# LSH-masked attention and a LayerNorm feed-forward block on one core: projection copies on GpSimd, warm-up products, memset gates on loads, and a new instruction order

## The chip, the core and the metric

The kernel runs on one core of a Trainium2 chip. The core has five instruction streams that run side by side and meet only at semaphores: TensorE (PE, matrix products into PSUM), VectorE (DVE), ScalarE (ACT), GpSimd (POOL) and SyncE (SP, which here does nothing but issue DMAs). The time is that of one execution on the device, in microseconds (us); the number compared is the median of the runs.

## The reference, cut to what matters

```python
# attention: q, k, v are (4, 8, 768, 64), proj is (64, 6)
q_bits = (einsum('bhsd,dk->bhsk', q, proj) > 0)
k_bits = (einsum('bhsd,dk->bhsk', k, proj) > 0)
mask = bucket(q_bits)[:, :, :, None] == bucket(k_bits)[:, :, None, :]
scores = where(mask, q @ k.T / 8, -1e9)
attn = softmax(scores);  attn_out = attn @ v
# block: x is attn_out as (4, 768, 512), w_ch1 (512, 2048), w_ch2 (2048, 512)
xn = (x - mean(x)) / sqrt(var(x) + 1e-6) * g_ln
out = x + maximum(xn @ w_ch1, 0) @ w_ch2
```

## The kernel before

The work is cut into 12 query units `u` (three blocks of 256 queries for each of the four batches) and, for attention, into 72 steps `s`: unit `s // 6`, head group `g` (four heads), key part `kp` (256 of the 768 keys). A batch's q and k come as f32 tiles `X` (one for each `g` and for q or k, `t` = 0 or 1), are transposed in blocks on DVE, cast to bf16 (`qb`, `kb`), and hashed: a product with the projection (`hf` or `hp`), then the sign as +0.5 or -0.5 (`G`). The score product adds the hash product to q times k, so that equal buckets come out far above all others and no mask is needed.

Every operation is one word of a long string, `ORDER`: its name, the engine, and its indices. The program plays the words one after the other, so the order of the words is the order of the instructions on each engine; no scheduler moves anything. In the profile a row names the line of the instruction, inside the function; below, the line where the function begins. The words that matter here:

- `lx` (L294) loads part of an `X` tile of batch 0, `LX` (L408) a whole one of a later batch, `lv` (L370) v, `lw1` and `lw2` (L359, L362) a quarter of a weight matrix each, from GpSimd's queue, with a cast to bf16.
- `tn` (L299) transposes one third of an `X` tile of batch 0 into a `tp` tile (three buffers); `ca` (L306) casts it into `qb` or `kb`.
- `ha` (L316) is the hash product of batch 0 with the block-diagonal projection `pfull` (written by `pf`, L281); `bh` (L320) takes the signs. For the query blocks that are needed later, `hc` (L326) uses the column-tiled projection `p32` instead, and `bc`, `sl`, `bi` spread the result. `hm` (L418) is the hash product of a later batch, also with `p32`; `mo` (L434) are the 16 small DMAs for each group that put its signs in place.
- `tu` (L411) and `CA` (L415) are transposes and casts of the later batches (`T`, two buffers).
- `p32` (L285) is four small copies of the projection, one for each 32 partitions. They stand on DVE.
- `S` (L447) is the score product of a step into two PSUM tiles, `E` (L464, on ACT) the exponential of each half, `A` (L467) the product with v. The first three steps take their PSUM tiles from three in rotation; all others share two, `scA` and `scB`, so that `S` of a step overwrites what `E` of the step before reads.
- `na`, `nb`, `nc`, `ce` (DVE) normalise and centre a unit, `rs` (POOL) makes the inverse deviation, `fl` a DMA transpose (`ft` and `fc` for unit 0).
- `F` (L526) and `R` are the first feed-forward product and its relu, `D` (L543) the second, `Z` the sum with x, `O` the store.
- `warm` (L289) is 32 products of ones before the first real one.
- `mem` and `pmem`, `sel`, `on`, `cv` and `su` fill constants, the spread matrix, the ones column, v in bf16 and the sums of v.

Of the kernel before, what the change touches and what calls it, by code (L numbers as in the profile page):

```python
# [19 lines left out]
mem.v lp.a tab.a lx.s.1.0.0.1 tn.v.1.0.0 lx.s.0.0.0.1 pf.v ca.p.1.0.0 warm.t ha.t.1.0.0 tn.v.0.0.0 ha.t.0.0.0  # L20
lx.s.0.1.1.3 lx.s.0.1.0.1 bh.v.1.0.0 lx.s.1.1.0.3 lx.s.0.0.1.3 tn.v.0.1.2 bh.v.0.0.0 sel.p on.p.0 tn.v.0.1.1
ha.t.0.1.2 bh.v.0.1.2 ha.t.0.1.1 bh.v.0.1.1 ca.a.0.0.0 ca.p.0.1.2 lv.s.0.0.4 on.p.1 lv.s.0.4.4 ca.p.0.1.1 tn.v.0.1.0
S.t.2.2 tn.v.1.1.0 ha.t.0.1.0 bh.v.0.1.0 ca.p.1.1.0 tn.v.1.1.1 E.a.2.0 ca.v.0.1.0 tn.v.0.0.1 E.a.2.1 S.t.1.2 E.a.1.0
ca.p.1.1.1 E.a.1.1 ha.t.1.1.1 lw1.p.3 S.t.0.2 E.a.0.0 tn.v.1.1.2 lx.s.1.0.1.3 E.a.0.1 ha.t.1.1.0 bh.v.1.1.1 pmem.p
S.t.4.2 E.a.4.0 p32.v hc.t.0.0.1 E.a.4.1 ca.a.0.0.1 bh.v.1.1.0 ha.t.1.1.2 bh.v.1.1.2 cv.p.0.0.2 tn.v.1.0.2 cv.p.0.0.0
A.t.2.2 S.t.3.2 bc.v.0.0.1 cv.p.0.4.0 E.a.3.0 sq.t.0.0 LX.s.1.0.1 E.a.3.1 tn.v.1.0.1 sl.t.0.0.1 sc.v.0.0 bi.a.0.0.1
A.t.0.2 LX.s.1.0.0 tu.v.1.0.1.0 ca.p.1.1.2 S.t.5.2 E.a.5.0 lw1.p.2 lg.s hc.t.1.0.2 E.a.5.1 tn.v.0.0.2 cv.p.0.4.2
sq.t.0.4 sc.a.0.4 A.t.1.2 na.v.0.0 LX.s.1.1.1 ca.v.1.0.1 S.t.8.2 A.t.5.2 nb.v.0.0 E.a.8.0 hc.t.0.0.2 tu.v.1.0.0.3
A.t.3.2 E.a.8.1 bc.v.0.0.2 sl.t.0.0.2 tu.v.1.0.1.3 bi.a.0.0.2 A.t.4.2 na.v.0.1 lw1.p.0 nb.v.0.1 S.t.6.2 hc.t.1.0.1
bc.v.1.0.1 E.a.6.0 bc.v.1.0.2 A.t.8.2 LX.s.1.1.0 lv.s.1.4.1 E.a.6.1 sl.t.1.0.1 bi.a.1.0.1 nc.v.0.1 lv.s.1.0.3  # L30
nc.v.0.0 S.t.7.2 A.t.6.2 ce.v.0.0 lw1.p.1 E.a.7.0 E.a.7.1 ft.t.0.0 fc.a.0.0 ce.v.0.1 sl.t.1.0.2 bi.v.1.0.2 ft.t.0.1
fc.v.0.1 S.t.9.2 tu.v.1.0.0.2 A.t.7.2 E.a.9.0 E.a.9.1 rs.p.0 lv.s.1.0.1 F.t.0.7 na.v.1.0 F.t.0.6 lw2.p.0 tu.v.1.0.1.2
R.a.0.7 R.a.0.6 nb.v.1.0 ca.v.0.0.2 tu.v.1.0.1.1 lw2.p.1 S.t.10.2 E.a.10.1 E.a.10.0 lv.s.1.4.3 lw2.p.2 tu.v.1.0.0.1
F.t.0.5 F.t.0.4 R.a.0.4 CA.v.1.0.1 A.t.9.2 tu.v.1.0.0.0 lw2.p.3 S.t.11.2 hm.t.1.0 tu.v.1.1.0.3 bt.v.1.0 mo.s.1.0.2.3
A.t.10.2 mo.s.1.0.0.2 E.a.11.0 nc.v.1.0 mo.s.1.0.2.2 E.a.11.1 tu.v.1.1.0.2 R.a.0.5 S.t.14.2 E.a.14.0 E.a.14.1
mo.s.1.0.2.1 A.t.11.2 mo.s.1.0.3.2 mo.s.1.0.1.1 F.t.0.2 R.a.0.2 na.v.1.1 nb.v.1.1 F.t.0.3 R.a.0.3 S.t.12.2
tu.v.1.1.0.1 A.t.14.2 nc.v.1.1 ce.v.1.0 ce.v.1.1 CA.p.1.0.0 tu.v.1.1.0.0 fl.s.1.0 CA.v.1.1.0 F.t.0.0 mo.s.1.0.0.1
E.a.12.0 fl.s.1.1 ca.v.1.0.2 F.t.0.1 E.a.12.1 A.t.12.2 tu.v.1.1.1.0 R.a.0.0 tu.v.1.1.1.1 mo.s.1.0.0.3 LX.s.2.0.0
R.a.0.1 mo.s.1.0.3.3 mo.s.1.0.3.0 tu.v.1.1.1.2 S.t.13.2 E.a.13.0 E.a.13.1 mo.s.1.0.0.0 D.t.0.0.0 D.t.0.0.1 D.t.0.0.2
tu.v.1.1.1.3 hm.t.1.1 S.t.16.2 E.a.16.0 bt.v.1.1 CA.p.1.1.1 mo.s.1.1.3.1 E.a.16.1 F.t.1.2 A.t.13.2 lv.s.1.0.2  # L40
mo.s.1.1.3.3 mo.s.1.0.1.3 D.t.0.0.3 R.a.1.2 lv.s.1.0.0 su.p.1.0 tu.v.2.0.0.2 S.t.15.2 E.a.15.1 mo.s.1.1.0.2
LX.s.2.0.1 mo.s.1.0.1.2 Z.v.0.0 F.t.1.4 R.v.1.4 D.t.0.1.0 D.t.0.1.1 mo.s.1.0.1.0 rs.p.1 mo.s.1.1.0.0 LX.s.2.1.0
mo.s.1.0.3.1 mo.s.1.1.2.0 tu.v.2.0.0.1 F.t.1.1 E.a.15.0 mo.s.1.0.2.0 R.a.1.1 cv.p.1.0.2 S.t.17.2 E.a.17.0 na.v.2.0
A.t.16.2 F.t.1.5 D.t.0.1.2 lv.s.1.4.2 tu.v.2.0.1.1 E.a.17.1 mo.s.1.1.3.2 mo.s.1.1.1.1 mo.s.1.1.2.2 S.t.18.2 R.v.1.5
D.t.0.1.3 mo.s.1.1.1.0 mo.s.1.1.1.2 E.a.18.1 A.t.17.2 F.t.1.0 E.a.18.0 A.t.15.2 cv.p.1.0.0 R.a.1.0 S.t.20.2 E.a.20.0
F.t.1.3 R.a.1.3 lv.s.1.4.0 cv.p.1.4.0 Z.v.0.1 E.a.20.1 tu.v.2.0.1.0 D.t.1.0.0 D.t.1.0.1 LX.s.2.1.1 nb.v.2.0 F.t.1.6
mo.s.1.1.1.3 na.v.2.1 S.t.19.2 nb.v.2.1 cv.p.1.4.2 nc.v.2.1 tu.v.2.0.0.3 R.v.1.6 mo.s.1.1.2.1 nc.v.2.0 A.t.20.2
mo.s.1.1.0.3 mo.s.1.1.0.1 on.p.2 E.a.19.1 F.t.1.7 tu.v.2.0.1.2 mo.s.1.1.2.3 tu.v.2.0.0.0 mo.s.1.1.3.0 A.t.18.2
tu.v.2.0.1.3 D.t.1.0.2 E.a.19.0 S.t.21.2 lv.s.2.0.0 R.a.1.7 D.t.1.0.3 ce.v.2.0 fl.s.2.0 ce.v.2.1 E.a.21.1 Z.v.1.0
fl.s.2.1 hm.t.2.0 bt.v.2.0 mo.s.2.0.0.1 mo.s.2.0.2.1 E.a.21.0 S.t.22.2 CA.a.2.0.0 sp.t.1.0 rs.p.2 mo.s.2.0.2.0  # L50
D.t.1.1.0 tu.v.2.1.1.0 LX.s.3.0.0 CA.p.2.0.1 mo.s.2.0.3.3 A.t.19.2 sc.a.1.0 na.v.3.0 F.t.2.0 lv.s.2.0.2 tu.v.2.1.0.0
D.t.1.1.1 mo.s.2.0.0.3 mo.s.2.0.1.3 E.a.22.0 E.a.22.1 R.a.2.0 tu.v.2.1.1.3 su.p.1.4 S.t.23.2 lv.s.2.4.3 sp.t.1.4
mo.s.2.0.1.1 D.t.1.1.2 sc.v.1.4 LX.s.3.0.1 E.a.23.0 F.t.2.1 E.a.23.1 R.v.2.1 D.t.1.1.3 mo.s.2.0.3.0 S.t.24.2 E.a.24.0
tu.v.2.1.0.1 F.t.2.5 O.s.0.3 A.t.23.2 O.s.0.1 A.t.22.2 R.v.2.5 tu.v.2.1.1.1 E.a.24.1 Z.v.1.1 F.t.2.3 R.a.2.3 S.t.26.2
E.a.26.0 lv.s.2.4.1 E.a.26.1 lv.s.2.0.3 O.s.1.3 nb.v.3.0 nc.v.3.0 lv.s.2.4.0 mo.s.2.0.3.2 A.t.21.2 tu.v.2.1.0.2
F.t.2.2 D.t.2.0.0 S.t.25.2 E.a.25.1 R.v.2.2 na.v.3.1 F.t.2.4 R.a.2.4 tu.v.2.1.0.3 CA.v.2.1.0 D.t.2.0.1 A.t.24.2
E.a.25.0 F.t.2.6 R.a.2.6 nb.v.3.1 nc.v.3.1 ce.v.3.1 S.t.29.2 lv.s.2.0.1 E.a.29.0 cv.p.2.0.2 O.s.1.1 LX.s.3.1.1
A.t.26.2 D.t.2.0.2 E.a.29.1 F.t.2.7 O.s.1.0 O.s.0.0 fl.s.3.1 S.t.28.2 R.a.2.7 tu.v.2.1.1.2 E.a.28.1 D.t.2.0.3
hm.t.2.1 ce.v.3.0 E.a.28.0 mo.s.2.0.2.3 mo.s.2.0.2.2 fl.s.3.0 Z.v.2.0 mo.s.2.0.3.1 S.t.31.2 E.a.31.1 tu.v.3.0.0.3
mo.s.2.0.0.0 lv.s.2.4.2 bt.v.2.1 E.a.31.0 A.t.25.2 su.p.2.0 mo.s.2.1.1.0 mo.s.2.1.2.0 na.v.4.0 cv.p.2.4.0 D.t.2.1.0  # L60
sp.t.2.0 A.t.29.2 sc.v.2.0 A.t.28.2 O.s.1.2 S.t.27.2 E.a.27.1 E.a.27.0 F.t.3.4 R.v.3.4 D.t.2.1.1 nb.v.4.0 CA.p.2.1.1
mo.s.2.0.1.0 F.t.3.7 R.v.3.7 S.t.30.2 nc.v.4.0 A.t.27.2 E.a.30.0 na.v.4.1 F.t.3.1 R.v.3.1 mo.s.2.1.3.1 mo.s.2.1.2.1
nb.v.4.1 nc.v.4.1 tu.v.3.0.1.1 ce.v.4.1 D.t.2.1.2 LX.s.3.1.0 E.a.30.1 ce.v.4.0 mo.s.2.1.2.3 S.t.32.2 E.a.32.0
A.t.31.2 mo.s.2.0.1.2 F.t.3.2 E.a.32.1 D.t.2.1.3 tu.v.3.0.0.2 S.t.35.2 R.a.3.2 F.t.3.0 E.a.35.0 R.v.3.0 rs.p.4
E.a.35.1 Z.v.2.1 A.t.32.2 O.s.0.2 A.t.30.2 F.t.3.6 mo.s.2.1.3.3 R.v.3.6 S.t.34.2 E.a.34.0 D.t.3.0.0 mo.s.2.1.0.2
mo.s.2.1.1.3 F.t.3.3 cv.p.2.0.0 na.v.5.0 A.t.35.2 E.a.34.1 R.v.3.3 S.t.33.2 mo.s.2.1.1.2 F.t.3.5 su.p.2.4 fl.s.4.1
E.a.33.0 rs.p.3 D.t.3.0.1 R.v.3.5 D.t.3.0.2 D.t.3.0.3 O.s.2.1 sp.t.2.4 mo.s.2.1.0.1 E.a.33.1 lv.s.3.4.3 lv.s.3.4.0
# [51 lines left out]
def kernel(  # L119
# [15 lines left out]
    nc = tc.nc  # L135
    P = 128
# [473 lines left out]
```

## Time and profile before

| | |
|---|---|
| median of 3 runs | 311.44 us (310.58 to 312.64) |
| profiled execution: time, span | 312.11 us, 310.4 us |
| PE busy | 297.2 us (96%) |
| ACT busy | 189.2 us (61%) |
| DVE busy | 175.5 us (57%) |
| POOL busy | 77.2 us (25%) |
| mean granted TensorE clock | 0.988 |

The span runs from the first to the last instruction of the profiled execution; what the run takes beyond it (1.7 us) lies around it. Busy shares are means over the span. A busy PE is not a PE at full rate: the ends of matmuls are modelled, and the clock granted to TensorE can be halved for a while.

### The profile page before, as it was taken

How to read it: one execution, taken by the hardware profiler on the slowest of the kernel's cores; microseconds unless marked ns; L12 is line 12 of the kernel's file. 1: busy time of each engine (PE TensorE's matmuls, PEld its weight loads, DVE VectorE, ACT ScalarE, POOL GpSimd, SP SyncE). 2: the span in 40 equal slices, each digit the busy share in tenths (PEclk: the TensorE clock that was granted, in tenths of full speed). 3: DMA queues.
4: the chain of work that ended last, by engine and by line, in shares of the span. 5: the costliest groups of instructions: out<-in, count | busy, mean ns of one | idle time of the engine just before them, and what ended most of it. 6: DMA issues, size and time to landing. Idle time of an engine off the chain costs nothing.

```text
span 310.4 us, 9968 instructions
## 1 busy us (share of the span) xinstructions
PE 297.2 (96%) x4410; PEld 206.2 (66%) x4410; DVE 175.5 (57%) x353; ACT 189.2 (61%) x211; POOL 77.2 (25%) x95
## 2 busy tenths in 40 slices
PE   7959899999999999999999999999999999999995
PEld 6636677666756767766776766676776676676663
DVE  3784964933865966836867634436474246356112
ACT  2475778766685786666866677557667577332220
POOL 3590055017270152630100005096101001001000
PEclk9998979999999999999999999999999999999999
DMA  6999979148446955130252222420310311103122
GB/s 194 373 303 229 301 124 178 40 138 254 134 65 221 264 121 162 44 88 2 55 94 73 20 55 57 84 55 5 87 36 2 85 38 34 36 2 82 55 68 68
DMA packets 30426, 33.58 MB, mean 108 GB/s; under 512 B 15536, under 2 KB 27056, under 8 KB 30384
## 3 DMA queue, kind: packets, MB, share of 16 engines
q1 hardware_dynamic: 25792, 28.50, 33.5%
q0 software_dynamic: 4224, 4.19, 8.5%
q8 instruction: 34, 0.56, 0.8%
q10 hardware_dynamic: 368, 0.26, 0.3%
q14 instruction: 8, 0.07, 0.1%
HBM read 27.53 MB, written 6.29 MB: 109 GB/s over the span
## 4 chain that ended last, share of the span: by engine, by line
PE 85%; DVE 6%; DMA 3%; POOL 2%; ACT 2%; issue 1%; SPq 0%; DVEq 0%
PE f L531 26%; PE sc L459 16%; PE acc L474 11%; PE hf L318 3%; DMA X<-in_q_dram 3%; PE hp L423 2%; ACT E L465 2%; DVE T L242 1%; DVE p L287 1%; POOL qb L251 1%; PE f_01None L547 1%; PE f_80None L547 1%; PE f_31None L547 1%; PE f_101None L547 1%; PE f_100None L547 1%; PE f_20None L547 1%
## 5 line engine op out<-in xcount | busy, mean ns | idle before, releaser
L465 ACT ACTIVATE E<-sc,bias_sb 128x1024 bf16<-128x1024 f32 x144 | 153.6, 1111 | 71.8 <-PE sc L459 71.8
L531 PE MATMUL f<-xnT,w_sb 128*128 128x256 bf16 x768 | 99.4, 273 | 0.3 <-DVE B L245 0.3
L531 PEld LDWEIGHTS <-w_sb 128*128 128x128 bf16 x768 | 71.1, 98 | 20.9 <-issue 6.1
L547 PEld LDWEIGHTS <-hb 128*128 128x128 bf16 x400 | 37.1, 98 | 31.7 <-issue 3.8
L541 DVE TENSOR_SCALAR hb<-f 128x512 bf16<-128x512 f32 x45 | 31.0, 688 | 44.8 <-PE f L531 44.4
L459 PE MATMUL sc<-qb,kb 32*128 32x256 bf16 x1152 | 53.7, 271 | 0.3 <-issue 0.3
L539 ACT ACTIVATE hb<-f 128x512 bf16<-128x512 f32 x51 | 30.3, 596 | 31.9 <-PE f L531 30.2
L474 PEld LDWEIGHTS <-E 128*128 128x128 bf16 x1152 | 42.0, 99 | 8.0 <-issue 4.8
L474 PE MATMUL acc<-vaug,E 128*128 128x65 bf16 x1152 | 46.0, 195 | 0.0
L459 PE MATMUL sc<-G 6*128 6x256 bf16 x576 | 42.9, 276 | 1.4 <-ACT E L465 1.4
L509 POOL TENSOR_SCALAR rs<-mv 128x2 f32<-128x2 f32 x12 | 7.1, 593 | 103.5 <-DVE mv L503 103.2
L242 DVE STREAM_TRANSPOSE T<-X 128x384 f32<-128x384 f32 x48 | 26.1, 561 | 12.0 <-POOL qb L251 4.2
L459 PEld LDWEIGHTS <-kb 32*128 32x128 bf16 x1152 | 30.8, 95 | 2.4 <-issue 0.5
L459 PEld LDWEIGHTS <-G 6*128 6x128 bf16 x576 | 15.6, 92 | 21.9 <-issue 19.9
L487 DVE SCALAR_TENSOR_TENSOR y<-vsB,acc 128x520 f32<-128x520 f32 x24 | 16.5, 688 | 16.8 <-PE acc L474 14.8
L376 POOL CAST vaug<-vn 128x768 bf16<-128x768 f32 x16 | 13.3, 851 | 37.3 <-DMA vn<-in_v_dram 20.6
L384 POOL TENSOR_TENSOR t<-vn 128x768 f32<-128x768 f32 x6 | 10.9, 1810 | 40.7 <-DMA G<-B 33.0
L504 DVE SCALAR_TENSOR_TENSOR xc<-x,mv,gB 128x512 bf16<-128x512 f32 x24 | 19.7, 820 | 0.9
L500 DVE BATCH_NORM_STATS2 st<-x 128x6 f32<-128x256 f32 x48 | 17.5, 414 | 0.4
L496 DVE TENSOR_TENSOR x<-y,rc 128x512 f32<-128x512 f32 x24 | 16.8, 699 | 1.1 <-DVE rc L494 0.3
L318 PE MATMUL hf<-tp,pfull 128*128 128x256 f32 x32 | 10.4, 469 | 1.6 <-DVE pfull L283 1.2
L242 DVE STREAM_TRANSPOSE tp<-X 128x256 f32<-128x256 f32 x24 | 9.0, 417 | 3.0 <-DMA X<-in_q_dram 2.8
(107 smaller groups left out, 244.1 us busy)
## 6 DMA issues: line engine op xcount, KB each, us to landing
out_dram<-x SPq DMA_DIRECT2D x44, 128.0 KB
X<-in_k_dram SPq DMA_DIRECT2D x7, 768.0 KB
X<-in_q_dram SPq DMA_DIRECT2D x6, 768.0 KB
vn<-in_v_dram SPq DMA_DIRECT2D x24, 192.0 KB
w_sb<-in_moe_w_ch_dram POOLq DMA_DIRECT2D x8, 512.0 KB, 10.6
vn<-in_v_dram SPq DMA_DIRECT2D x2, 768.0 KB
G<-B SPq DMA_DIRECT2D x96, 4.5 KB
X<-in_q_dram SPq DMA_DIRECT2D x2, 512.0 KB
```

Of the source, the lines that this page charges most:

```text
L242: nc.vector.transpose(d[:, j], s[:, j, kj0 : kj0 + n])
L318: nc.tensor.matmul(hf(g, t, kp)[:, :256], pfull[:, j], tp(g, t, kp)[:, j], start=(j == 0), stop=(j == 1))
L459: nc.tensor.matmul(sc(s, i // 2)[:, i % 2, 256 * kk : 256 * kk + 256], lh, rh, start=(rep == 0), stop=(rep == 2), skip_group_check=True,)
L465: nc.scalar.activation(E(s)[:, heads(h)], sc(s, h), AF.Exp, scale=EXP_SCALE, bias=bias_sb)
L474: nc.tensor.matmul(acc[:, qt, (D + 1) * i : (D + 1) * (i + 1)], E(s)[:, i, 256 * kk + P * qt : 256 * kk + P * qt + P], vaug(u // 3)[:, 4 * ...
L496: nc.vector.tensor_tensor(xo, a[:, :, :, 0:D], rc.to_broadcast([P, 2, 4, D]), op=AOP.mult)
L500: nc.vector.bn_stats(stats(u)[:, qt, g], xt(u)[:, qt, 256 * g : 256 * g + 256])
L504: nc.vector.scalar_tensor_tensor(xc(u)[:, t], xt(u)[:, t], mv(u)[:, t, 0:1], gB, op0=AOP.subtract, op1=AOP.mult,)
L531: nc.tensor.matmul(f1[:, n].rearrange("p (t x) -> p t x", t=2), w1_sb[:, dt, P * nt : P * nt + P], xnT(u)[:, :, dt], start=(dt == 0), stop ...
L539: nc.scalar.activation(hb(u)[:, 2 * p : 2 * p + 2], f1, AF.Relu)
L541: eng.tensor_scalar_max(hb(u)[:, 2 * p : 2 * p + 2], f1, 0.0)
L547: nc.tensor.matmul(f2, hb(u)[:, nt, P * t : P * t + P], w2_sb[:, nt, half(h)], start=(nt == 0), stop=(nt == NNT - 1),)
```

## The change

`wm` is a new word: four more products of ones into the PSUM tile of `warm`. Eight of them stand among the first hash products. `gx` is a new word: a memset of one column of an `X` tile, on POOL or DVE; it stands ahead of each of the four loads `LX` of batch 1, which overwrite the same tile and so wait for the memset. `p32` stands on POOL. The whole order is new; its beginning is shown, once as it was (first lines) and once as it is, and no other function is touched. The line numbers of the new file are 1 higher in the order's wake, 5 higher behind `wm` and 8 higher behind `gx`.

```diff
 ORDER = """
-mem.v lp.a tab.a lx.s.1.0.0.1 tn.v.1.0.0 lx.s.0.0.0.1 pf.v ca.p.1.0.0 warm.t ha.t.1.0.0 tn.v.0.0.0 ha.t.0.0.0
-lx.s.0.1.1.3 lx.s.0.1.0.1 bh.v.1.0.0 lx.s.1.1.0.3 lx.s.0.0.1.3 tn.v.0.1.2 bh.v.0.0.0 sel.p on.p.0 tn.v.0.1.1
-ha.t.0.1.2 bh.v.0.1.2 ha.t.0.1.1 bh.v.0.1.1 ca.a.0.0.0 ca.p.0.1.2 lv.s.0.0.4 on.p.1 lv.s.0.4.4 ca.p.0.1.1 tn.v.0.1.0
-S.t.2.2 tn.v.1.1.0 ha.t.0.1.0 bh.v.0.1.0 ca.p.1.1.0 tn.v.1.1.1 E.a.2.0 ca.v.0.1.0 tn.v.0.0.1 E.a.2.1 S.t.1.2 E.a.1.0
-ca.p.1.1.1 E.a.1.1 ha.t.1.1.1 lw1.p.3 S.t.0.2 E.a.0.0 tn.v.1.1.2 lx.s.1.0.1.3 E.a.0.1 ha.t.1.1.0 bh.v.1.1.1 pmem.p
-S.t.4.2 E.a.4.0 p32.v hc.t.0.0.1 E.a.4.1 ca.a.0.0.1 bh.v.1.1.0 ha.t.1.1.2 bh.v.1.1.2 cv.p.0.0.2 tn.v.1.0.2 cv.p.0.0.0
+mem.v lp.a tab.a lx.s.0.0.0.1 lx.s.0.1.1.3 lx.s.0.1.0.1 lx.s.1.0.0.1 lx.s.1.1.0.3 lv.s.0.0.4 warm.t wm.t.0 wm.t.1
+tn.v.0.0.0 lx.s.0.0.1.3 ca.a.0.0.0 wm.t.2 pf.v tn.v.0.1.2 ca.p.0.1.2 wm.t.3 wm.t.4 lg.s ha.t.0.0.0 bh.v.0.0.0 wm.t.5
+wm.t.6 on.p.0 ha.t.0.1.2 tn.v.0.1.1 ha.t.0.1.1 lx.s.1.0.1.3 ca.p.0.1.1 bh.v.0.1.2 tn.v.0.1.0 S.t.2.2 lv.s.0.4.4
+E.a.2.0 wm.t.7 E.a.2.1 bh.v.0.1.1 p32.p ha.t.0.1.0 bh.v.0.1.0 S.t.1.2 E.a.1.0 gx.p.1.0.1 tn.v.1.1.1 ha.t.1.1.1
+lw1.p.3 E.a.1.1 ca.v.0.1.0 bh.v.1.1.1 tn.v.1.0.0 S.t.0.2 ca.p.1.1.1 ca.p.1.0.0 ha.t.1.0.0 LX.s.1.0.1 E.a.0.0
+tn.v.1.1.0 ha.t.1.1.0 bh.v.1.0.0 S.t.4.2 E.a.0.1 cv.p.0.0.0 cv.p.0.0.2 E.a.4.0 tn.v.0.0.1 hc.t.0.0.1 lw1.p.2
+tn.v.1.1.2 bh.v.1.1.0 E.a.4.1 ca.a.0.0.1 bc.v.0.0.1 A.t.0.2 ca.v.1.1.0 ha.t.1.1.2 sel.p lv.s.1.4.1 gx.v.1.0.0
+bh.v.1.1.2 S.t.3.2 sq.t.0.0 lv.s.1.4.2 E.a.3.0 tn.v.0.0.2 E.a.3.1 LX.s.1.0.0 sl.t.0.0.1 A.t.1.2 bi.a.0.0.1 tn.v.1.0.2
+ca.p.1.1.2 S.t.5.2 hc.t.1.0.2 A.t.2.2 ca.v.1.0.2 lw1.p.0 cv.p.0.4.2 cv.p.0.4.0 tn.v.1.0.1 lw1.p.1 lv.s.1.0.2
+ca.p.1.0.1 sc.v.0.0 na.v.0.0 E.a.5.0 ca.p.0.0.2 lv.s.1.0.0 sq.t.0.4 E.a.5.1 S.t.8.2 sc.a.0.4 hc.t.0.0.2 E.a.8.0
+tu.v.1.0.1.2 A.t.4.2 E.a.8.1 A.t.3.2 nb.v.0.0 bc.v.0.0.2 A.t.5.2 bc.v.1.0.2 gx.p.1.1.1 lv.s.1.0.3 sl.t.0.0.2
...
+LX.s.1.1.1 E.a.6.1 S.t.7.2 sl.t.1.0.2 nc.v.0.1 lw2.p.0 lw2.p.2 bi.v.1.0.1 A.t.6.2 E.a.7.0 ce.v.0.0 bi.v.1.0.2
+ft.t.0.0 ce.v.0.1 ft.t.0.1 fc.v.0.0 E.a.7.1 fc.v.0.1 S.t.9.2 E.a.9.0 tu.v.1.0.0.3 A.t.7.2 gx.v.1.1.0 F.t.0.6
...
+    def wm(eng, n):
+        for _ in range(4):
+            nc.tensor.matmul(made["warm"][:, 0, :P], ones, ones, start=True, stop=True)
+
...
+    def gx(eng, b, g, t):
+        eng.memset(Xt(b, g, t)[:, 0:1], 0.0)
```

In numbers of words, over the whole program: `S`, `E`, `A`, `F`, `R`, `D`, `O`, `mo`, `tu` and the loads are as many as before, and each as often on its engine; of the twelve `CA`, seven stand on DVE (four before), four on POOL (five) and one on ACT (three).

## The prediction

> **What bounds the kernel now.** I read the page first: the busy shares, and the span in slices. PE and the granted clock are:
>
> ```profile
> span 310.4 us, 9968 instructions
> PE 297.2 (96%) x4410; PEld 206.2 (66%) x4410; DVE 175.5 (57%) x353; ACT 189.2 (61%) x211; POOL 77.2 (25%) x95
> ...
> PE   7959899999999999999999999999999999999995
> ...
> PEclk9998979999999999999999999999999999999999
> ```
>
> PE is full from the fourth slice on; what can be won lies in the first fifth and in the tail. To size it I counted whole words against their full-rate rows in the chain of waits: `S` 0.77, `A` 0.49, `F` 0.87, `D` 0.87, `hm` 1.44, `ha` 0.85 us (four passes 0.213 apart). Ahead of the first `D`, which starts at 59.19, stand 15 `S`, 14 `A`, 8 `F`, 8 `ha`, one `hm` and some 4.3 us of small products: 11.6 + 6.9 + 7.0 + 6.8 + 1.4 + 4.3 = 38 us. So 21 us were lost by then, 5.9 of them ahead of the first `ha`. From there to the last product at 306.6 PE only pays for changes of operand.
>
> The timeline and the list of what PE waited for show where the rest went:
>
> ```profile
> 12.35 8.25 ACT L465 ACTIVATE E<-sc,bias_sb 128x1024 bf16<-128x1024 f32 x8 [5.04 <-PE sc L459]
> 17.27 4.47 DVE L287 COPY p<-prj 32x12 f32<-32x12 f32 x4
> ...
> 17.48 2.37 POOL L376 CAST vaug<-vn 128x768 bf16<-128x768 f32 x3
> 19.80 1.05 POOL L253 CAST kb<-tp 128x512 bf16<-128x512 f32 x1
> ...
> 21.80 0.43 PE L329 MATMUL hf<-tp,p 128*32 128x64 f32 x16 [3.32 <-DVE p L287]
> ...
> 26.08 2.12 ACT L465 ACTIVATE E<-sc,bias_sb 128x1024 bf16<-128x1024 f32 x2 [4.96 <-PE sc L459]
> ...
> 29.10 2.12 ACT L465 ACTIVATE E<-sc,bias_sb 128x1024 bf16<-128x1024 f32 x2 [0.63 <-PE sc L459]
> ```
> ```profile
> 20.00:25.00 5.00, 3.18 (x48) 2.39 (x52) 3.38 (x10) 1.12 (x2) 3.85 (x5) 0.79 1.03 239
> ```
>
> The first of the four `p32` copies lasts 3.61 us on DVE, from 17.27 to 20.88; its three sisters last 0.16, 0.48 and 0.17. It ends 0.03 us behind the last of four POOL casts that run without a gap from 17.48 to 20.85. Meanwhile `hc.0.0.1` stands at the head of PE, and behind it `S.3`, whose exponential is late by 4.96 us. The idle stretch also costs clock: the column ahead of DMA in the second fence is the granted clock, and it is half from 22.92 to 26.34.
>
> Before the first `F` (42.82) PE isn't the limit anyway: `E.3`, `E.5`, `E.8`, `E.6`, `E.7` start at 26.08, 29.10, 32.05, 35.12 and 38.08, 3.0 us apart, though two halves last 2.12. Each `S` must wait for both halves of the step before, in the same two PSUM tiles.
>
> **The change, part by part.** The order before the first `D` is nearly the same on PE, so I walk the new one with the rows of the old.
>
> *Start.* Transfers land one after the other: 256, 256, 512 and 256 KB at 4.15, 5.00, 7.31 and 8.14. The new order of loads (256 of q, 512 and 256 of k, group 0) puts the k that the first step needs at 6.5 and 7.3. On PE 32 products of ones took from 1.11 to 4.67, 0.107 apart at half clock; 20 more follow at once, to 6.7, or to 6.3 if the clock is released on the way. Before, the clock was released at 9.27 only; PE had been busy 71% of the 3.41 us up to 5.86, and idle from 4.67 to 5.91. Now nothing is idle there. With `ha` at 0.85 and DVE's chain (transposes 0.77, signs 0.42): `ha.0.0.0` 6.3, third part of k transposed 7.3, signs 7.75, second part 8.55, signs 9.0, `ha.0.1.1` to 9.45, `S.2` at 9.5. It was 11.48: minus 2.0. If the clock still waits until 9.27, `ha` is 1.71 twice, and `S.2` is at 11.05: minus 0.4. I take the 2.0, since the added products fill just the gap. The other three `wm` groups (0.22 us each) lie in waits for transposes; laid bare they cost 0.7.
>
> *To `E.4`.* DVE has to do, from 11.9 on, the transposes 111, 100 and 110, the cast of k (0.61), signs twice, and 0.65 of waits for products between: 16.35. POOL casts k twice (1.07 each), sets the ones (0.55), copies `p32`, issues `lw1.3` (1.0), casts k (1.07) and scales q (1.51): it ends at 16.5, since q's transpose is ready at 14.95 only. `S.4` runs 16.65 to 17.4 and `E.4` starts then; before, 18.49.
>
> *`p32` on POOL.* The trace has no such copy on POOL. From below, the memset of 128x2, 0.13; from above the smallest arithmetic, 0.79 (`rs`). Four are 0.5 to 3.2 us; I take 0.3 each, nearest the small memsets, thus 1.2. They end by 11.3 (13.3 by the upper end), and `hc.0.0.1` asks at 17.4: nothing on the path, because POOL would only wait for a transpose until 12.7 (bare, it would hold q's scaling by 1.2 to 3.2). DVE is rid of 4.5 us, and of the block.
>
> *To `E.3`.* `S.3` can finish when `E.4` is done, 19.5, plus 0.75: 20.3, if its k cast (`ca.v.1.1.0`, DVE, 18.55) is free. It was 26.08: minus 5.8. That DVE cast and `ca.v.1.0.2` are of the kind that was blocked, and now stand beside POOL's runs. My walk puts them into POOL's weight issues, beside which the later `p32` copies ran unhindered; a miss costs up to 2.2 us (four selects of 0.30 and a cast of 1.07), a hit nothing. I carry 0.3. [...]
>
> *POOL's reload.* The built program has an instruction that reloads POOL's library ahead of the first scaling of q. Before, it stood first, at 0.80, under an idle stretch until 5.04; now it stands behind the cast of `ca.p.1.1.1`, at about 13.7. That row bounds it: the scaling began 0.09 after its transpose, so at most 4.2, at least 0. I take 0, as the operation lasted no longer than 1.51, which fits the 4.12 of three times its size. At 4.2, q's scaling ends 19.4, `E.4` starts 20.2, and 2.8 us of the gain go. [...]
>
> *To the first `F`.* Three-us steps: `E.7` at 32.3, ended 34.4, then `S.9` and `A.7` at 0.77 and 0.49: `F` at 35.8 at full clock, 37.0 at the half clock that the old one had there (39.99 to 43.40). It was 42.82. I take 6.3 of the 5.8 to 7.0, less the 0.3.
>
> *To `D.0.0.0` and beyond.* Same words, one `A` fewer (0.5, given back later): `D.0.0.0` at 59.19 − 6.0 − 0.5 = 52.7. w2 must be there. The four quarters of w1 took 25.7 us from the first issue at 16.18 to the last landing at 41.87, those of w2 another 13.0. From 12.5 on that gives 38.2 for w1 and 44.7 for the w2 quarter that `D.0.0.0` reads: 8 to spare, so only a gain of over 14 would meet the loads. `CA` of group 0 on DVE (0.96 and 0.91) takes the place of POOL's 4.12, for which DVE waited 4.2; DVE has room. Afterwards, changes into `A` from another word, 0.10 each, rise from 45 to 50: plus 0.5. The old order had one late stall of 0.52; for the new one I allow 0.5 more.
>
> *Gates.* Four memsets of one column, 0.06 to 0.13. What they move are loads: `LX.1.0.1` 12.7 to 11.7, `LX.1.0.0` 17.1 to 19.4, `LX.1.1.1` 25.7 to 27.8, `LX.1.1.0` 28.6 to 36, behind `fc` on DVE. SP queues behind the last: six `mo`, `LX.2.0.1`. The `mo` wait for `hm.1.0` (42.6) anyway. Cover: `LX.1.1.0` took 7.5 from issue to landing, so 43.5; DVE asks at 43.2. Hidden, just.
>
> Sum: 6.0 − 0.5 (changes into `A`) − 0.5 (late stall) = 5.0; with everything in place (full clock at the first `F`, no late stall) 7. I take 5.6. The profiled 312.11 becomes 306.5; the median of the runs is 0.67 below that execution, so 305.8.
>
> **The rivals.** *POOL holds the start* (a reload of up to 4.2, or a blocked DVE cast): 2.2 to 2.8 of the 5.6 go: 308.0 to 308.6. For: POOL's queue is fuller early, and `tp` has only three buffers, so DVE waits for POOL's casts. Against: the reload row shows no cost.
>
> *The gain is given back.* PE is 96% busy; a new order may pay the 5.6 in small waits between words: 311.4. For: 240 us of new order; against: the old one shows 0.5 of waits there.
>
> *Slower: the last gated load.* `tu.1.1.0.2` stands on DVE right behind the signs of group 0, and behind it the relus, `na.1.1` and `ce.1.0`. If `LX.1.1.0` isn't landed at 43.2, DVE stops and PE with it, as soon as its PSUM tiles are full. The weights' fourth quarter took 18.8 us from issue to landing under full queues. With that, it lands at 54.8: 11.6 of stall, less about 1 that ACT's relus cover, minus 5.6: 5 slower, 316.4. It outweighs the gain once the landing takes over 14 us. For: w2 is queued ahead; against: the 7.5 of the same load under w1.
>
> **How the numbers follow.** The forecast has 0.55 (302.5 to 308), POOL 0.20, given back 0.12, slower 0.13. The likeliest gives 305.8. The range goes from 302.5 (all terms at their good ends) to 312.0, leaving out the slower rival and a little below. About 1% (3.1 us) can be told from no change, so faster by over 1% means under 308.3: the forecast and most of POOL, 0.72; slower over 314.6, 0.13; the rest 0.15.
>
> **What would show it.** Right: `hc` without a wait on `p32`; first `E` near 10.3, `E.3` near 20, first `F` near 36, first `D` near 52; PE full from then on. Wrong: a gap on POOL of several us ahead of the first scaling of q; a DVE cast of 512 columns over 1 us; DVE idle for `X` near 43; PE idle after 60.

## The result, and the profile after

The changed kernel takes 308.38 us (median of 4 runs, 307.36 to 308.77), the kernel before on the same chip 312.02 us (4 runs, 310.58 to 312.64). The ratio is 0.9885, with a 95% interval of 0.9838 to 0.9932: some 3.6 us are gained, where 5.6 were forecast. Medians here are over all runs of a kernel; ratios leave out disturbed executions.

Page after, from its head and from the span in 40 slices (7.7 us each):

```profile
span 306.8 us, 10039 instructions
...
PE 296.4 (97%) x4442; PEld 206.7 (67%) x4442; DVE 173.0 (56%) x357; ACT 186.7 (61%) x205; POOL 78.1 (25%) x101
...
PE   8998899999999998999999999999999999999993
...
PEclk9999599999999999999999999999999999999998
```

The hole in PE's third slice (5 tenths before) is closed. A new one stands in the clock: the fifth slice (31 to 38 us) ran at half. The last slice shows 3 tenths instead of 5: the tail without products has become longer.

The timeline after, where the exponentials of the first steps start and where `p32` went (start, duration, engine, instruction; in brackets the idle time before it and its releaser):

```profile
9.86 0.88 POOL L288 COPY p<-prj 32x12 f32<-32x12 f32 x4
...
10.28 6.20 ACT L473 ACTIVATE E<-sc,bias_sb 128x1024 bf16<-128x1024 f32 x6 [4.62 <-PE sc L467]
...
17.28 2.12 ACT L473 ACTIVATE E<-sc,bias_sb 128x1024 bf16<-128x1024 f32 x2 [0.80 <-PE sc L467]
...
17.82 0.64 DVE L254 CAST kb<-tp 128x512 bf16<-128x512 f32 x1
...
20.30 2.12 ACT L473 ACTIVATE E<-sc,bias_sb 128x1024 bf16<-128x1024 f32 x2 [0.38 <-PE sc L467]
...
31.67 0.38 PE L482 MATMUL acc<-vaug,E 128*128 128x65 bf16 x7 [1.56 <-issue]
```

The four copies last 0.88 together on POOL, and no product waits for them. `E.2` starts at 10.28 (12.35 before), `E.4` at 17.28 (18.49), `E.3` at 20.30 (26.08). The last row is new: in the middle of `A.8` PE stopped for 1.56 us, and "issue" means that nothing in the profile was waited for. The list of PE's waits and the windows (the column ahead of DMA and GB/s is the granted clock) show what followed:

```profile
PE acc L482 <- issue: 1.6, 1, 1.6
PE warm L293 <- DVE bias_sb L259: 1.1, 1, 1.1
PE f L539 <- DVE hb L549: 1.0, 1, 1.0
```
```profile
30.00:35.00 5.00, 3.44 (x63) 2.59 (x59) 3.64 (x10) 2.84 (x4) 1.46 (x3) 0.70 1.13 295
35.00:40.00 5.00, 4.88 (x60) 3.56 (x59) 3.67 (x9) 2.89 (x3) 1.85 (x3) 0.61 1.22 215
```

Directly behind the stop the clock is half for 6.83 us, from 32.03 to 38.86. The first `F` comes at 38.12 (42.82 before), the first `D` at 53.54 (59.19). The third wait is one `F` that waits for a relu on DVE until 116.47. The chain of waits leads back from there to a load of v (start, duration, what):

```profile
93.79 8.35 DMA vn<-in_v_dram
...
103.11 1.79 POOL t L389
...
106.78 1.64 POOL t L389
...
111.14 4.09 POOL qb L252
115.26 0.07 DVE T L243
115.32 0.43 issue
115.76 0.66 DVE hb L549
116.47 1.03 PE f L539 x8
```

POOL waits for v, then sums it twice (`su`), then scales q (`CA.p.2.1.0`, 4.09). DVE's next transpose needs the buffer that this scaling reads, and the relu `hb` stands on DVE behind the transpose. In the kernel before this word was `CA.v.2.1.0`: the change itself moved it from DVE to POOL.

PE's last product ends at 301.93 (306.57 before), so 4.64 us were won up to there. The span is 3.57 shorter only: from the last product to the end it is now 4.90, and was 3.84.

### The profile page after: what moved, and what is told of

The parts are those of the page before. It is cut to its first block, busy times and chain, and to the rows that moved or that the text cites. A ratio compares the mean times of both kernels' runs of the same rounds, so it can differ in the third digit from the quotient of the medians.

```text
span 306.8 us, 10039 instructions
## 1 busy us (share of the span) xinstructions
PE 296.4 (97%) x4442; PEld 206.7 (67%) x4442; DVE 173.0 (56%) x357; ACT 186.7 (61%) x205; POOL 78.1 (25%) x101
## 4 chain that ended last, share of the span: by engine, by line
PE 76%; POOL 7%; DMA 4%; SPq 4%; DVE 4%; issue 2%; ACT 1%; POOLq 0%
PE f L539 24%; PE sc L467 14%; PE acc L482 10%; DMA vn<-in_v_dram 3%; PE hp L431 2%; POOL qb L252 2%; SPq L443 2%; DMA X<-in_k_dram 2%; PE hf L323 1%; POOL vaug L381 1%; SPq L378 1%; PE f_31None L555 1%; PE f_00None L555 1%; PE f_101None L555 1%; PE f_100None L555 1%
## 5 line engine op out<-in xcount | busy, mean ns | idle before, releaser
L555 PEld LDWEIGHTS <-hb 128*128 128x128 bf16 x400 | 37.2, 98 | 31.8 <-issue 3.5
L549 DVE TENSOR_SCALAR hb<-f 128x512 bf16<-128x512 f32 x45 | 30.9, 687 | 36.4 <-PE f L539 35.8
L467 PE MATMUL sc<-G 6*128 6x256 bf16 x576 | 42.1, 276 | 0.6 <-ACT E L473 0.6
L512 DVE SCALAR_TENSOR_TENSOR xc<-x,mv,gB 128x512 bf16<-128x512 f32 x24 | 18.0, 752 | 0.8
L246 DVE TENSOR_SCALAR B<-hp 128x384 bf16<-128x384 f32 x6 | 3.3, 558 | 10.7 <-PE hp L431 10.0
```

The costliest lines, as they stand in the source:

```text
L467: nc.tensor.matmul(sc(s, i // 2)[:, i % 2, 256 * kk : 256 * kk + 256], lh, rh, start=(rep == 0), stop=(rep == 2), skip_group_check=True,)
L512: nc.vector.scalar_tensor_tensor(xc(u)[:, t], xt(u)[:, t], mv(u)[:, t, 0:1], gB, op0=AOP.subtract, op1=AOP.mult,)
L549: eng.tensor_scalar_max(hb(u)[:, 2 * p : 2 * p + 2], f1, 0.0)
L555: nc.tensor.matmul(f2, hb(u)[:, nt, P * t : P * t + P], w2_sb[:, nt, half(h)], start=(nt == 0), stop=(nt == NNT - 1),)
```

## The experiments

### p32 on POOL alone, in the kernel before

```diff
-... S.t.4.2 E.a.4.0 p32.v hc.t.0.0.1 ...
+... S.t.4.2 E.a.4.0 p32.p hc.t.0.0.1 ...
```

> The kernel before, with the four p32 copies moved from DVE to POOL and every other word where it was. Theory (most of the gain is the copy that was held for 3.61 us): hc.0.0.1 no longer waits 3.32 us, E.3 comes some 4 us earlier (near 22 instead of 26.08), the half-clock stretch from 22.92 to 26.34 is gone, and the kernel takes 3 to 4.5 us less than before: 307.5 to 309 against 312.0. Rival (the gain comes from the new order of loads and the warm-up products): this change alone is worth at most 1 us, 311 to 312. Rival (the wait is only replaced: POOL's casts of v and k come later by the copies): E.3 gains 2 or less and the time 1 to 2, 310 to 311.

Measured: 307.05 us (306.07 to 308.16), ratio 0.9871 (0.9822 to 0.9920). Its timeline:

```profile
17.36 0.91 POOL L286 COPY p<-prj 32x12 f32<-32x12 f32 x4
...
18.32 0.43 PE L328 MATMUL hf<-tp,p 128*32 128x64 f32 x16
...
21.50 2.12 ACT L464 ACTIVATE E<-sc,bias_sb 128x1024 bf16<-128x1024 f32 x2 [0.51 <-PE sc L458]
```

One letter gives the whole gain. `hc` runs at 18.32 instead of 21.80, `E.3` at 21.50 instead of 26.08; the first `F` is at 37.00, the first `D` at 53.34, the tail 3.82. From 9.05 to the tail the clock is full. So all the rest of the change (new order of loads, `wm`, `gx`, the order anew) brings nothing that can be told in the total: the ratios 0.9871 and 0.9885 lie in each other's interval. It does start the first step 1.94 us earlier (`E.2` 10.28 against 12.22); at the first `D` the two are 0.20 apart, and at the end the changed kernel's profiled span is 1.6 us longer. What eats the 1.94 is the next question.

### The place of p32: earlier on DVE, and back on DVE in the changed kernel

```diff
 kernel before:
-... pf.v ... E.a.4.0 p32.v ...
+... pf.v p32.v ... E.a.4.0 ...
 changed kernel:
-... bh.v.0.1.1 p32.p ha.t.0.1.0 ...
+... bh.v.0.1.1 p32.v ha.t.0.1.0 ...
```

> The kernel before, with the p32 copies still on DVE but moved to the place right behind pfull's copies. Theory (it was the place beside POOL's unbroken run of casts, not the engine): the copies last 0.2 to 0.5 each, the start is later by 0.7 to 1 us, the 3.3 us wait of hc.0.0.1 is gone, and the time is 2.5 to 4 less than before: 308 to 309.5. Rival (a DVE copy of this kind is slow whenever POOL works): POOL scales q there from 5.04 to 6.55, so one copy would last over 1 us, the first score step would come some 1.5 us late, and the time would be 1 to 2 less than before at best: 310 to 311.

> The changed kernel with p32 back on DVE at the new place, ahead of the last signs of the first key part. Theory (place, not engine): POOL ends a cast at 9.92 and then only sets one column and issues a weight load, and DVE is idle from 9.94 to 11.53, so the four copies last 0.2 to 0.5 each and hide: the time is that of the changed kernel within 0.5, 308 to 309. Rival (the engine matters): one copy lasts over 1 us, the signs at 11.53 come late and the time is 1.5 to 3.5 above the changed kernel.

Measured: 308.22 us (306.73 to 309.58), ratio 0.9895 (0.9828 to 0.9962), for the first; 311.78 (307.46 to 314.87, 10 runs), 0.9954 (0.9907 to 1.0002), for the second. The copies in the timeline of the first, and of the second:

```profile
4.93 1.51 POOL L250 TENSOR_SCALAR qb<-tp 128x512 bf16<-128x512 f32 x1 [4.44 <-DVE tp L241]
...
5.78 1.24 DVE L286 COPY p<-prj 32x12 f32<-32x12 f32 x4
```
```profile
10.02 1.00 POOL L364 DMA_DIRECT2D w_sb<-in_moe_w_ch_dram  x1
...
10.16 1.01 DVE L287 COPY p<-prj 32x12 f32<-32x12 f32 x4
```

Neither set is held: the longest single copy is 0.51 beside POOL's scaling and 0.50 beside its weight issue. `hc` waits for the copies in neither. So it was the place, not the engine; that much of the theory holds. The first moved `E.2` by 0.22 only (12.57 against 12.35), where 0.7 to 1 was expected; but PE stopped there too, for 1.39 us at 34.13 with nothing waited for, and the clock was half from 37.64 to 41.05. The time of the second was expected at 308 to 309 and is not: `E.3` is at 20.48, as in the changed kernel, but in the profiled run PE stopped for 2.08 us at 30.1 and waited 2.71 for a relu, until 118.8. Both are places where the changed kernel itself loses, and no copy of `p32` is near. Its ten runs spread over 7 us, so its time says little on `p32`.

### Is it the unbroken run of POOL casts? A weight issue put into the run

```diff
-... cv.p.0.0.2 ... cv.p.0.0.0 ... cv.p.0.4.0 ... ca.p.1.1.2 ... lw1.p.2 ...
+... cv.p.0.0.2 lw1.p.2 ... cv.p.0.0.0 ... cv.p.0.4.0 ... ca.p.1.1.2 ...
```

> The kernel before with its transposing transfers as plain copies (the transposition of the normalised x is left out for units 1 to 11; all of them stand behind 45 us), p32 still on DVE at its place; the one edit that matters here: POOL's issue of the weight quarter lw1.2, which takes 0.79 us and stood behind the run of four casts, is moved into that run, behind its first cast (so lw1.2 is also issued some 2.5 us earlier). Theory (the copy is shut out for as long as POOL casts follow each other without a gap, and slips in at the first gap): the first p32 copy ends when the first cast ends, so it lasts about 1.0 us instead of 3.61, and its three sisters run during the issue; hc.0.0.1 waits under 1 us, E.3 comes 2.5 us earlier or more. Rival (the copy is long for a reason of its own, or merely slowed by traffic of any kind): it stays over 3 us.

Measured: 313.85 us (2 runs), ratio 1.0103 (1.0049 to 1.0157). This kernel also has plain copies in place of the transposing transfers, and the kernel before with these alone was not run, so the total belongs to both edits; the rows below lie ahead of any of these transfers.

```profile
17.34 5.34 DVE L286 COPY p<-prj 32x12 f32<-32x12 f32 x4
...
17.55 0.85 POOL L375 CAST vaug<-vn 128x768 bf16<-128x768 f32 x1
...
18.32 0.79 POOL L359 DMA_DIRECT2D w_sb<-in_moe_w_ch_dram  x1
...
19.11 1.60 POOL L375 CAST vaug<-vn 128x768 bf16<-128x768 f32 x2
...
20.65 1.05 POOL L252 CAST kb<-tp 128x512 bf16<-128x512 f32 x1
...
21.65 0.82 POOL L375 CAST vaug<-vn 128x768 bf16<-128x768 f32 x1
```

The first row starts ahead of the casts, as before, and at 5.34 it is 0.87 longer than before, not shorter. Singly the four copies last 1.80, 2.59, 0.75 and 0.17 us, and `hc` waits 4.20. The first ends at 19.14, the second at 21.74, the third at 22.50: each within 0.04 of the end of POOL's instruction (issue to 19.11, cast to 21.71, cast to 22.47). That a copy beside these casts is held up to a boundary of POOL is shown, and so is that it has no length of its own. The expected 1.0 us for the first was wrong: the gap behind the first cast did not free it, it waited through the issue too, and its sisters then met the other casts. A gap does not mend the place; it exposes more copies. In the kernel before, three copies that *started* during an issue ran at 0.16 to 0.48.

### Without the extra warm-up products

```diff
-... warm.t wm.t.0 wm.t.1 tn.v.0.0.0 ...   (and six more wm words)
+... warm.t tn.v.0.0.0 ...
```

> The changed kernel without the eight groups of four extra warm-up products. Theory A (they release the clock: 4.73 after, 9.27 before): PE is idle from 4.6 to 5.7, the granted clock stays at half until about 9, each ha of the start takes 1.7 instead of 0.85, S.2 starts near 11 instead of 9.40, and the time is 1 to 1.6 above the changed kernel: 309.4 to 310. Theory B (the transfers and DVE set the start, and the clock is released anyway): S.2 within 0.3 of 9.4 and the time within 0.5 of 308.4. Beside that PE's stop of 1.56 at 30.11 to 31.67, in which it waited for nothing the profile shows while an instruction packet of 16 KB was moving: if it hangs on the place in the instruction stream, it moves by the 32 products left out, to a word later, or vanishes, with up to 1.5 of gain.

Measured: 308.42 us (306.93 to 312.08), ratio 0.9898 (0.9829 to 0.9967). In the profiled run the clock was released at 4.24 without them, and `E.2` started at 10.15. The stop in mid-run shrank to 0.26, no clock was lost, and the first `F` came at 35.95, where the prediction had it:

```profile
32.15 0.29 PE L466 MATMUL sc<-qb,kb 32*128 32x256 bf16 x3 [0.26 <-issue]
```

By this one execution `wm` would be useless at the start and harmful at 30 us. The next kernels test the second half, and a later one corrects the first.

### The same number of PE instructions without the words: 64 products in the warm-up

As in the run with the gap, the transposing transfers are plain copies in all that follow. These kernels leave out the transposition of the normalised x in units 1 to 11 and so do not compute the reference; they serve for times alone. First the changed kernel as it is, the base:

```diff
-        eng.dma_start_transpose(out=xnT(u)[:, t], in_=xc(u)[:, t])
+        eng.dma_start(out=xnT(u)[:, t], in_=xc(u)[:, t].rearrange("p (c x) -> p c x", c=NDT))
```

> The changed kernel with its 22 transposing transfers (fl) written as plain copies from xc to xnT; the transposition of the normalised x is left out for units 1 to 11, everything else and every word's place is kept. It is the base for the kernels that follow with a p in front. All fl stand behind 44 us, so up to the first F it is the changed kernel: first E near 10.3, E.3 near 20.3, first F between 36 and 38. Time if the transfers are hidden anyway: that of the changed kernel within 1 us, 307 to 309.5; if they were late for some F: 1 us or more less.

Then the warm-up:

```diff
-NWARM = 32
+NWARM = 64      (and no wm words)
```

> p_after without the wm words but with 64 instead of 32 products of ones in the first warm-up, so that PE's stream has as many instructions ahead of the first step as in the changed kernel. Theory (PE runs out of instructions near 30 us: in three traces its stop ended 1.55 to 1.58 us behind the end of a 16 KB instruction packet, and 64 instructions more, products and their weight loads, bring that point forward): the stop of 1 to 2 us at 30 to 32 is back, a stretch at half clock follows it, and the first F starts near 38 as in the changed kernel, where it was at 35.95 without the wm words. Rival (the stop falls by chance, or is caused by the place of the wm words): no stop, first F near 36, some 0.3 later for the longer warm-up at the start.

Measured: base 310.26 us (305.93 to 312.56, 10 runs), 0.9950 (0.9898 to 1.0002); with 64 products 310.31 (306.91 to 315.81), 0.9957 (0.9904 to 1.0009). The base's interval overlaps that of the changed kernel, so what the plain copies do to the total can't be told. The stop is back in the same place:

```profile
31.89 0.55 PE L481 MATMUL acc<-vaug,E 128*128 128x65 bf16 x7 [2.29 <-issue]
```

Half clock follows for 10.24 us, and the first `F` is at 38.60. The words' place is thus not the cause. The table has every profiled execution of the changed kernel and its variants, with two variants of the kernel before at the end; "packet" is the end of the 16 KB transfer on the instruction queue that landed before PE resumed.

| kernel | stop, us | packet ended | PE resumed | at half clock, 31 to 42 | first `F` |
|---|---|---|---|---|---|
| changed | 1.56 | 30.12 | 31.67 | 6.83 | 38.12 |
| `p32` back on DVE | 2.08 | 30.64 | 32.21 | 6.83 | 38.17 |
| base with plain copies | 2.18 | 30.53 | 32.18 | 3.41 | 37.47 |
| 64 products, no `wm` | 2.29 | 30.42 | 31.89 | 10.24 | 38.60 |
| no `gx` | 2.18 | 29.93 | 31.50 | 3.41 | 37.15 |
| tail and `CA` | 1.50 | 29.78 | 31.15 | 3.41 | 36.44 |
| `CA` alone | 1.74 | 29.70 | 31.15 | 3.41 | 36.63 |
| no `wm` | 0.26 | 30.79 | 32.15 | none | 35.95 |
| no `wm`, tail and `CA` | 0.76 | 31.93 | 33.45 | 6.83 | 38.41 |
| the same, 16 products | 0.64, 1.27 | 27.22, 33.95 | 28.70, 35.44 | none | 37.47 |
| `p32` on POOL alone | 0.22 | 32.09 | 33.67 | none | 37.00 |
| `p32` early on DVE | 1.39 | 33.94 | 35.52 | 3.41 | 39.81 |

In all thirteen stops PE resumes 1.36 to 1.65 us behind the end of such a packet. The kernel before stopped in the same way for 0.27 (1.54 behind a packet) and the kernel with the gap for 0.76 (1.74). The seven kernels with the larger number of instructions stop 1.50 to 2.29 us, those with fewer 0.22 to 1.39. The transfer queue row of the changed kernel counts these packets:

```profile
q8 instruction: 35, 0.57, 0.8%
```

The 8884 products and weight loads of PE, over 35 packets of 16 KB, are 254 for each. I read the stop as PE running out of instructions while the queues are full of data (DMA share 1.13, 295 GB/s in that window). A count in the traces agrees with this reading: in all fourteen executions, whatever the word, 961 of PE's instructions (955 to 957 products and weight loads, the rest of its sequencer) stand ahead of the stop, and the other stop of the kernel with 16 products has 705 ahead of it, 256 fewer. That the packet carries the instructions that PE lacks is inferred from these counts; no row shows it. The packet began to move only when 891 to 942 of the 961 had started, and it took 0.88 to 1.30 us. Without `wm` and its 64 instructions the 961 reach further into the program: PE comes to the stop at 31.89 instead of 30.11, when the packet has landed (30.79). What makes one packet later than another is not settled: 32 products fewer still did not take the last stops away.

### Without the gates on the loads

```diff
-gx.p.1.0.1  gx.v.1.0.0  gx.p.1.1.1  gx.v.1.1.0
```

> p_after without the four gx memsets; the loads of batch 1 then wait only for the last reader of their tile. Theory (the gates are worth nothing on this path): the time is that of p_after within 1 us, the loads are issued 0 to 8 us earlier, LX.1.1.0 by most. Rival A (the gates help, since they hold these loads back behind the weights and v): the weight quarters of w1 and w2 or the v tiles land 2 us later or more, and a product waits for one: 1 us or more slower. Rival B (the last gate costs, since it holds LX.1.1.0 and what is queued behind it on SP): 0.5 to 1 us faster.

Measured: 311.71 us (307.52 to 315.00, 10 runs), ratio 0.9962 (0.9896 to 1.0027), against 0.9950 of the base. `LX.1.1.0` is issued at 25.0 instead of 37.2 and lands at 39.8 instead of 45.1; the other three are issued 0.6 to 3.0 earlier; the last quarter of w2 lands at 51.95 (51.57 in the base). No product waits for any of these, and the two ratios lie in each other's interval: the gates are worth nothing that can be told, as the theory had it, though the spread leaves room for half a per cent either way. Its profiled run waited 3.30 us for a relu, until 117.5; kernels with the gates had the same wait, of 2.71 at most. That is the next question.

### The late stall and the tail

```diff
-CA.p.2.1.0
+CA.v.2.1.0
```

with, in the first of the two, also the words from `D.10.1.3` to the end in the old pattern:

```diff
-... D.t.11.1.0.1 D.t.11.1.1.1 D.t.11.1.2.1 D.t.11.1.3.1 ... Z.v.11.1.1 ... D.t.11.1.2.0 D.t.11.1.3.0 Z.v.11.1.0 ...
+... D.t.11.1.2.0 ... D.t.11.1.3.0 ... Z.v.11.1.0 ... D.t.11.1.0.1 D.t.11.1.1.1 ... D.t.11.1.2.1 D.t.11.1.3.1 Z.v.11.1.1 ...
```

> p_after with two edits far apart: the words from D.10.1.3 to the end in the pattern of the kernel before, and CA.2.1.0 on DVE instead of POOL. Theory: (1) the span ends 3.8 to 4.0 us after PE's last product instead of 4.90, since one of the last half's six stores on SP waited there for an earlier store's semaphore; (2) PE's stall of 0.99 at 116.5 falls away, because DVE no longer stands behind POOL's 4.11 us scaling of q (on DVE it would take about 1). Together 1.5 to 2 less than p_after. Rivals: (1) the tail only shifts, since PE's small products between the last F cost what the stores save: last product later by 0.5 to 1, no gain; (2) the stall stays, as the v load that landed at 102 holds POOL and with it the next sum.

> p_after with only CA.2.1.0 moved from POOL to DVE, the tail as in the changed kernel. Theory (the late stall is the larger part of what is missing: 0.8 to 3.3 us in six traces near 115 to 119, and a half-clock stretch behind it where it was 2.7 or more): no wait of F for hb near 115, the median 2 to 3 us under that of p_after (310.2 among its fast runs), 307.5 to 308.5, and the runs closer together; the tail from PE's last product to the end stays at 4.8 to 4.9. Rival (the tail's order was the larger part): within 1 us of p_after.

Measured: with both edits 306.73 us (305.64 to 308.59, 10 runs), 0.9885 (0.9842 to 0.9928); with `CA` alone 306.95 (306.10 to 309.70, 4 runs), 0.9896 (0.9844 to 0.9948). The base had 310.26. PE's waits with `CA` alone:

```profile
PE acc L481 <- issue: 1.7, 1, 1.7
PE warm L292 <- DVE bias_sb L258: 1.1, 1, 1.1
PE sc L466 <- ACT E L472: 0.9, 2, 0.6
PE hf L322 <- PE sc L466: 0.4, 2, 0.2
```

The wait for `hb` is gone from the list. In the six profiled executions of the changed kernel and its variants with this scaling on POOL it was 0.99, 2.71, 0.85, 1.80, 3.30 and 1.53 us, and where it reached 2.7 the clock went to half for 3.41 us as it ended (from 118.64 and 116.91). Of the base's ten runs seven are above 310 us; of the fourteen with `CA` on DVE none is above 309.7. So the one word takes the wait away, and the late runs are not seen again in these two kernels. That the stall, not the tail, was the larger part is likely, as the tail adds nothing that can be told to `CA` alone. The totals don't show it: the base's interval (0.9898 to 1.0002) overlaps both others, and a kernel of the next section, with the same word on DVE, has a run at 310.33. The timeline with both edits shows the same place:

```profile
110.41 1.02 POOL L516 TENSOR_SCALAR rs<-mv 128x2 f32<-128x2 f32 x1
...
110.42 0.92 DVE L251 TENSOR_SCALAR qb<-T 128x1536 bf16<-128x1536 f32 x1
...
111.28 0.69 DVE L548 TENSOR_SCALAR hb<-f 128x512 bf16<-128x512 f32 x1
```

The scaling that took 4.09 on POOL takes 0.92 on DVE, and the relu follows at once. The tail's order gives 4.26 us behind the last product instead of 4.81 (base) or 4.95 (`CA` alone), less than expected; the two kernels of the next section, with the same tail, have 4.68. In the total the two kernels differ by 0.2, so the tail's share can't be told; whether it only shifts stays open.

### All three together, and fewer warm-up products

```diff
-wm words, CA.p.2.1.0, new tail
+no wm words, CA.v.2.1.0, old tail      (second kernel: NWARM = 16)
```

> p_after without the wm words, with CA.2.1.0 on DVE and with the tail in the pattern of the kernel before. Theory: no stop over 0.5 us near 30 and no half-clock stretch at 32, so the first F starts near 36, the first D near 51; no stall near 115; tail near 4.25. That is 1.5 to 2.5 below the kernel with the last two edits alone (306.7): 304 to 305.5. Rival (the stop is chance): 306 to 307 as that kernel.

> The same with 16 instead of 32 products of ones in the first warm-up, so 32 instructions of PE fewer. Theory of the instruction stream: the little stop that was left without the wm words (0.26 at 32) goes too, and the first F is as early or 0.3 earlier, if the clock is still released in time; the time is within 0.5 of the kernel with 32. Rival (the warm-up is needed for the clock): the clock is released at 8 to 9 instead of 4.3, the first score step is 0.9 to 1.6 later, and the time is 1 to 1.6 above.

Measured: 307.91 us (305.41 to 310.33, 6 runs), 0.9888 (0.9841 to 0.9935), and 307.03 (305.75 to 309.25), 0.9899 (0.9853 to 0.9945). Both expectations failed: leaving `wm` out adds nothing to the two edits. In these executions the clock was released at 9.13 and 9.57, not at 4.24, and the first exponential started at 11.03 and 11.14. In the seven with `wm` or with 64 products it was released between 4.16 and 6.00, and the first exponential was between 9.63 and 10.46. The first exponential is 0.6 to 1.5 us earlier with them, and the single execution without `wm` had been lucky. But five of the seven releases came by 4.73, about when 32 products alone end (4.70); only those at 5.59 and 6.00 stand where the added products were running, so how often `wm` is what releases the clock stays open. And the first kernel of the two lost the clock near 33 although its stop was 0.76 only:

```profile
31.96 0.28 PE L466 MATMUL sc<-G 6*128 6x256 bf16 x2 [0.72 <-ACT E L472]
...
33.45 0.40 PE L466 MATMUL sc<-qb,kb 32*128 32x256 bf16 x3 [0.76 <-issue]
```

In the totals the warm-up's gain at the start and its cost at 30 us can't be told from nothing. No version was found that is told to be faster than `p32` on POOL alone (0.9871). The two edits in a kernel that keeps the transposing transfers were not run.

## Why the prediction was right, and where it missed

*Right by its steps up to `E.3`.* `S.2` at 9.40 (said 9.5), `E.4` at 17.28 (17.4), `E.3` at 20.30 (20.3), `p32` on POOL 0.88 (1.2, bounds 0.5 to 3.2), behind no wait. That the held copy was the price is shown by the run that moves it alone. The reload of POOL's library cost nothing visible: the scaling of q began at 14.79, lasted 1.52, and waited for its transpose. The DVE casts that might have been held lasted 0.64 and 0.43 us; the 0.3 carried for them was not needed. *POOL holds the start* did not happen. Part of the start was luck: the clock was released at 4.73, when the first 32 products had just ended, and the same start without `wm` had it at 4.24 once and at 9.13 once. The reading that PE was busy 71% of the 3.41 us up to 5.86 in the kernel before is off: the trace has 2.25 us, 66%; the idle gap that it points to is there.

*Mis-sized: "To the first `F`".* The working gave 35.8 to 37.0 and 6.3 us; the changed kernel reached 38.12 and 4.70. The term missing is PE's stop of 1.56, behind 961 of its instructions, and the half clock of 6.83 behind it. The steps themselves come every 3.0 us as said; where the stop was 0.26, `F` came at 35.95. The prediction held the half-clock end of its range for the price of the old window at 40; the new cause was not in it.

*Mis-sized: the choice of 5.6.* The sum was 5.0, and the good ends were given weight that the chip did not give. From the first `D` to the last product the forecast allowed 1.5 us of new loss (0.5 of `A` given back, 0.5 of changes, 0.5 of stall); it was 1.01 in the profiled execution, 248.39 against 247.38. But the late stall is 0.85 to 3.30 from run to run, so 0.5 was too little. The prediction priced the scalings of q that left POOL and not `CA.2.1.0`, which went from DVE to POOL and makes this stall. The 308.38 from four runs may sit on its lucky side: the base with plain copies has 310.26 over ten, 0.9950 with an interval up to 1.0002, which is no gain that can be told.

*Missing: the tail.* Nothing was said of the words behind the last `F`; it took 1.07 us. On the spans: 0.85 short at `D` (5.65 for 6.5), 0.49 won back up to the last product, 0.6 short by the choice and 1.07 by the tail, together the 2.03 between 5.6 and 3.57.

*The rivals.* The last gated load landed at 44.81, 1.3 later than said; DVE first read it at 46.46, as it was itself late, so the cover held and the slower rival did not come. *The gain is given back* is half right: the 1.94 at the start were given back, by the stop, the half clock, the late stall and the tail, as far as the profiled executions show, not by small waits between words. The copy's 4.6 at `E.3` stayed.

*Which POOL work held a copy.* Beside POOL's casts a copy lasted 3.61 us in the kernel before and 2.59 in the one with the gap, and 1.80 there beside a cast and a weight issue. Beside POOL's scaling the longest copy was 0.50 in the kernel before (scaling from 5.04 to 6.55) and 0.51 with `p32` early on DVE (from 4.93 to 6.44), each under a scaling of 1.51, which is no wait for the whole instruction.

## What to carry to other kernels

Look for small copies on DVE whose duration is many times that of their sisters (here 3.61 us against 0.16 to 0.48), and see what POOL did at the same time; move the copy to POOL or to a place where POOL is idle, and do that alone first. After a gain at the start, check PE for stops with no releaser (here 1.56 us) and the clock for stretches at half (6.83): products that fill a gap are instructions too, 64 here. When a kernel's runs spread by several us, look for the chain whose length varies with a load, here v, its sums and a scaling on POOL, and one transpose on DVE; one word on another engine took that wait (0.85 to 3.30 us) away. When a new order moves a long operation to another engine, price what waits behind it there: here a scaling that takes 0.92 us on DVE took 4.09 on POOL.

## What the runs showed of the hardware

- A DVE copy of 32x12 elements, 0.12 to 0.17 us while POOL was idle (`pfull` in the changed kernel, from 4.93 to 5.58), lasted 2.59 and 3.61 us beside POOL casts that followed each other without a gap, and 1.80 beside a cast and a weight issue; each ended within 0.04 us of an instruction boundary of POOL. POOL's `rs` near 110 us, 0.23 in seven executions, took 0.82 to 1.03 in the three in which it overlapped a scaling on DVE; but in the changed kernel it takes 0.77 to 0.78 in eight of its twelve places, so a hold in that direction is not shown by this alone. A DVE product of two f32 tiles took 1.06 us beside POOL's scaling (0.69 to 0.76 otherwise in that execution).
- PE's stops between 28 and 40 us that no engine's work explains ended 1.36 to 1.74 us behind a 16 KB instruction packet, in fifteen of fifteen, and stood behind 961 of its instructions in fourteen of them, behind 705 in the other.
- Ahead of the tail, the granted clock went to half in stretches of 3.41, 6.83 and 10.24 us. A stop of 1.5 us or more near 30 was followed by one in seven of seven; stops of 0.72 and 0.76 once too, and stops of 0.70 and 1.27 in another run not at all. At the start, products of ones stood 0.107 us apart up to the release of the clock and 0.056 behind it (the changed kernel, at 4.73). With the same 32 products, followed by about 1 us of idle PE, the release came at 4.24 in one execution and at 9.13 in another.
